# An S4D convolution and a SwiGLU FFN on one core: held loads, block 0's parameters apart, another instruction order

## The chip, the cores and the metric

The kernel runs on one core of a Trainium2 chip. The metric is the device time of one execution in microseconds (us), lower is better. A core has five engines that run on their own and meet at semaphores: TensorE (PE in the profile; its weight loads are PEld), VectorE (DVE), ScalarE (ACT), GpSimd (POOL) and SyncE (SP). Here SP only issues DMAs, and it issues all of them.

## The reference

Shapes: 2048 positions (L), 640 channels (D), 128 state pairs (N), FFN width 1728.

```python
def _A_ref(u, log_A_real, A_imag, C_real, C_imag, log_dt, D_skip):
    dt = jnp.exp(log_dt)
    A = -jnp.exp(log_A_real) + 1j * A_imag
    C = (C_real + 1j * C_imag) * dt[:, None]
    P = jnp.exp((A * dt[:, None])[:, :, None] * pos[None, None, :])
    K = 2.0 * jnp.einsum("dn,dnl->dl", C, P).real
    y = irfft(rfft(u_t, 2 * L) * rfft(K, 2 * L)[None], 2 * L)[:, :, :L]
    return y.transpose(0, 2, 1) + u * D_skip[None, None, :]

def _B_ref(x, w1, w3, w2):
    return (_silu(x @ w1) * (x @ w3)) @ w2

mod = (_silu(c) @ w_mod).reshape(1, 6, 1, -1)
sa, ca, ga, sb, cb, gb = (mod[:, i] for i in range(6))
h = _layernorm(x) * (1 + ca) + sa
x = x + ga * _A_ref(h, ...)
h = _layernorm(x) * (1 + cb) + sb
x = x + gb * _B_ref(h, B_w1, B_w3, B_w2)
```

## The kernel before

The channels are worked in five blocks of 128 (b = 0 to 4). For each block the kernel

- makes the tables of block b's phases on GpSimd (`t{b}.h.i`), and in eight chunks of 16 channels the convolution kernel's values: GpSimd adds the phases (`g{b}.{c}.ph`) and multiplies the magnitudes (`.z0` to `.z2`), ScalarE takes the sines (`.s0` to `.s4`), VectorE multiplies (`.m0` to `.m4`), TensorE sums over the state (`.p`, 32 fp32 products into `kps`), ScalarE copies the result out (`.r`), and VectorE adds the skip (`.d`)
- normalises the input (`h{b}.{i}.n`, on ScalarE or VectorE, four instructions of 128 x 128 for one of four tiles), multiplies and adds the modulation, and sends it through DRAM to another layout (`h{b}.f`)
- transforms both (`hh{b}.i.m` the input, `k{b}.i.m` the kernel; 16 products as the profile counts them, tile `ps`), applies the second step (`w{b}.i.f` and `.k`, tiles `fh` and `fk`), multiplies the spectra on VectorE (`.x0`, `.x1`, `.c`), and goes back (`z{b}.j.z`, tile `fz`), with a store of each part to the DRAM tensor `zd`.

Ahead of this stand the parameters: `in_log_ar`, `in_c_re`, `in_c_im`, `in_a_im` (128 partitions x 5 blocks x 128) are loaded whole, and VectorE and ScalarE make phases and magnitudes of them (steps `pa` for the phase, `pb` and `pc` for the magnitude and angle, `q` for the transposes). `al8{b}` multiplies a decay by 0 to 7, and `exp{b}` takes its exponentials.

All these steps are named tasks of one plan. `Plan.place` walks them with a cost for each and picks by rank. The ranks are the long table `RANKS`. A task may name two engines, and the plan takes the one that is to end first. The order that comes out is written into the program: each engine executes its instructions in exactly that order, SP its DMAs too. At most eight DMAs are in flight, since each waits for the one eight places ahead of it.

When the last chunk of block 4 is done, the task `change` frees the generator's pools, opens those of the FFN and loads the first 512 rows of x (`x2`, four DMAs of 320 KB) and a table `wd` (1 MB). Then `fw0` and `fw1` load the first two slices of FFN weights, `fs0` and `fs1` split them into two fp32r parts (ScalarE and VectorE), `iz0` and `iz1` load the back-transformed blocks 0 to 3, and `ir0` and `ir1` make the last step of the inverse transform for these rows (TensorE, then additions and statistics on VectorE). Block 4's part follows (`izb`), then the second layer norm, and the FFN: four groups of 512 rows, 14 slices each, every product in three fp32r products (`gu`, `acc`).

Of the kernel before, what the change touches and what calls it, by code (L numbers as in the profile page):

```python
# [18 lines left out]
P = 128  # L19
# [6 lines left out]
NB = 5  # L26
# [120 lines left out]
class InOrder:  # L147

    def __init__(self, k, eng):
        self.k, self.eng, self.prev = k, eng, None  # L150

    def __getattr__(self, name):
        f = getattr(self.eng, name)

        def g(*a, **kw):
            self.prev = self.k.order(f(*a, **kw), self.prev)  # L156
            return self.prev
# [120 lines left out]
class K:  # L278
# [534 lines left out]
    def run(self):  # L813
# [62 lines left out]
        z = {}  # L876
# [594 lines left out]
```

## Time and profile before

| | |
|---|---|
| median of three runs | 1010.73 us (1008.08 to 1012.32) |
| profiled execution | 1012.95 us, its span 1010.6 us |
| TensorE busy | 891.2 us, 88% of the span |
| VectorE busy | 656.8 us, 65% |
| ScalarE busy | 507.8 us, 50% |
| GpSimd busy | 279.4 us, 28% |
| DMA, over the span | 122.05 MB, mean 121 GB/s |

A row of groups reads: line, engine, operation, what it writes and reads, size, count | busy us, mean ns of one | idle time of the engine ahead of it, and who ended it. Since a helper records every operation, most rows have the helper's line, and it is the tile's name that tells them apart. A row of the timeline begins with the start and the duration in us; in brackets is the idle time before it and what ended it. A row of stretches has, for each engine, busy us and the number of instructions, then TensorE's granted clock (1.00 is full), the share of time that the DMA engines were busy, and GB/s.

### The profile page before, as it was taken

The numbers are of one execution on the slowest core, as the hardware profiler recorded it, in microseconds if no ns is written. First come the engines' busy times: TensorE is split into PE (matmuls) and PEld (weight loads), VectorE is DVE, ScalarE is ACT, GpSimd is POOL, SyncE is SP. The second block draws the span as 40 slices with busy tenths as digits, with TensorE's granted clock in tenths as the row PEclk, the third lists the DMA queues.
The fourth block names the chain that finished last, engine by engine and source line by source line (L and its number), as shares of the span: only waits on it lengthen the run. The fifth ranks groups of instructions, "written<-read, shape, count | busy, mean of one in ns | idle before, by whom it ended". The sixth has DMA issues, their size and how long they took to land.

```text
span 1010.6 us, 20260 instructions
## 1 busy us (share of the span) xinstructions
PE 891.2 (88%) x8129; PEld 714.0 (71%) x8129; DVE 656.8 (65%) x1214; ACT 507.8 (50%) x843; POOL 279.4 (28%) x288
## 2 busy tenths in 40 slices
PE   1463878788999885999999999999999999999996
PEld 1132756767887773677788888888888888888884
DVE  6998999999999475677664453464543643634332
ACT  6878787989787541432243343343433432533231
POOL 1798798988998200100000000000000000000000
PEclk9887998999999897899999999999999999999998
DMA  9955553624131759976232363332534333533302
GB/s 214 266 183 174 120 135 95 152 65 107 44 86 51 192 137 229 232 176 164 86 94 76 107 157 91 94 101 66 138 110 117 83 86 93 146 102 92 103 14 53
DMA packets 140998, 122.05 MB, mean 121 GB/s; under 512 B 13416, under 2 KB 124776, under 8 KB 139368
## 3 DMA queue, kind: packets, MB, share of 16 engines
q1 hardware_dynamic: 140904, 120.75, 45.4%
q8 instruction: 64, 1.05, 0.4%
q14 instruction: 30, 0.25, 0.1%
HBM read 99.75 MB, written 20.97 MB: 119 GB/s over the span
## 4 chain that ended last, share of the span: by engine, by line
PE 73%; DVE 12%; DMA 6%; ACT 3%; issue 3%; SPq 1%; POOL 0%; DVEq 0%; ACTq 0%; POOLq 0%
PE gu L753 12%; PE gu L754 12%; PE gu L755 12%; PE acc L788 6%; PE acc L789 6%; PE acc L790 6%; PE ps L156 4%; DVE yy L156 3%; PE fk L156 3%; PE kps L156 2%; PE fh L156 2%; DMA sp<-in_w_mod 2%; PE fz L156 2%; DVE fp L156 2%; PE iy L647 2%
## 5 line engine op out<-in xcount | busy, mean ns | idle before, releaser
L754 PE MATMUL gu<-xl,wh 128*128 128x512 f32 x540 | 212.6, 394 | 0.0
L753 PE MATMUL gu<-xh,wh 128*128 128x512 f32 x540 | 212.0, 393 | 0.5 <-ACT xh L683 0.5
L755 PE MATMUL gu<-xh,wl 128*128 128x512 f32 x540 | 211.7, 392 | 0.0
L658 ACT ACTIVATE wh<-wr 128x640 fp32r<-128x640 f32 x105 | 72.0, 732 | 136.3 <-PE gu L754 136.3
L721 POOL MEMSET w2l<- 64x640 f32 x3 | 1.9, 628 | 451.0 <-PE acc L789 451.0
L753 PEld LDWEIGHTS gu<-xh,wh 128*128 128x128 f32 x540 | 101.8, 188 | 25.6 <-issue 1.0
L754 PEld LDWEIGHTS gu<-xl,wh 128*128 128x128 f32 x540 | 101.9, 189 | 21.8
L755 PEld LDWEIGHTS gu<-xh,wl 128*128 128x128 f32 x540 | 101.8, 188 | 21.8
L788 PE MATMUL acc<-ah,w2h 128*128 128x512 f32 x260 | 103.8, 399 | 0.0
L789 PE MATMUL acc<-ah,w2l 128*128 128x512 f32 x260 | 102.2, 393 | 0.0
L768 DVE SCALAR_TENSOR_TENSOR a<-th,gu 128x512 f32<-128x512 f32 x52 | 35.8, 688 | 99.2 <-ACT th L767 99.0
L767 ACT ACTIVATE th<-gu 128x512 f32<-128x512 f32 x52 | 31.1, 598 | 135.4 <-PE gu L755 135.4
L769 DVE TENSOR_TENSOR a<-a,gu 128x512 f32<-128x512 f32 x52 | 35.7, 687 | 97.3 <-PE gu L755 97.2
L790 PE MATMUL acc<-al,w2h 128*128 128x512 f32 x260 | 96.5, 391 | 0.0
L156 POOL TENSOR_TENSOR yy<-e,e 128x512 f32<-128x512 f32 x80 | 86.3, 1095 | 16.6 <-PE kps L156 11.7
L659 DVE TENSOR_TENSOR wl<-wr,wh 128x640 fp32r<-128x640 f32 x105 | 82.2, 819 | 10.6 <-ACT wh L658 10.6
L156 POOL TENSOR_TENSOR ph<-p,p 128x1024 int32<-128x1024 int32 x40 | 79.0, 1975 | 7.3 <-ACT tr L156 6.6
L156 PE MATMUL kps<-yy,xx 128*32 128x64 f32 x2560 | 51.3, 234 | 31.3 <-DVE xx L156 23.4
L658 ACT ACTIVATE w2h<-w2r 128x640 fp32r<-128x640 f32 x51 | 37.6, 737 | 81.5 <-issue 42.6
L659 DVE TENSOR_TENSOR w2l<-w2r,w2h 128x640 fp32r<-128x640 f32 x51 | 42.0, 823 | 56.2 <-ACT w2h L658 56.0
L156 DVE TENSOR_TENSOR yy<-yy,tr 128x512 f32<-128x512 f32 (+1 forms) x80 | 75.5, 946 | 0.9 <-ACT tr L156 0.6
L156 PEld LDWEIGHTS kps<-yy,xx 128*32 128x32 f32 x2560 | 44.7, 116 | 41.2 <-issue 25.0
(204 smaller groups left out, 1646.6 us busy)
## 6 DMA issues: line engine op xcount, KB each, us to landing
wr<-in_w SPq DMA_DIRECT2D x104, 320.0 KB, 3.9
w2r<-in_w SPq DMA_DIRECT2D x52, 320.0 KB, 3.0
zd<-zt SPq DMA_DIRECT2D x40, 256.0 KB, 3.2
iz<-zd SPq DMA_DIRECT2D x24, 320.0 KB, 5.8
xs<-in_x SPq DMA_DIRECT2D x16, 320.0 KB, 11.4
hs<-hb SPq DMA_DIRECT2D x20, 256.0 KB, 2.4
xb<-hs SPq DMA_DIRECT2D x20, 256.0 KB, 4.8
x<-in_x SPq DMA_DIRECT2D x16, 320.0 KB, 11.0
```

The source lines that it names most:

```text
L156: self.prev = self.k.order(f(*a, **kw), self.prev)
L658: self.nc.scalar.activation(H, v, AF.Copy)
L659: eng.tensor_tensor(Lo, v, H.bitcast(F32), op=ALU.subtract)
L753: nc.tensor.matmul(pg, wh[:, i, k, :], xh[:, k, :], start=(k == 0), stop=False)
L754: nc.tensor.matmul(pg, wh[:, i, k, :], xl[:, k, :], start=False, stop=False)
L755: nc.tensor.matmul(pg, wl[:, i, k, :], xh[:, k, :], start=False, stop=(k == KT - 1))
L767: nc.scalar.activation(th, gu[0], AF.Tanh, scale=0.5)
L768: nc.vector.scalar_tensor_tensor(a, th, 1.0, gu[0], op0=ALU.add, op1=ALU.mult)
L769: nc.vector.tensor_mul(a, a, gu[1])
L788: nc.tensor.matmul(acc[k], w2h[:, sl], ah, start=(m == 0), stop=False)
L789: nc.tensor.matmul(acc[k], w2l[:, sl], ah, start=False, stop=False)
L790: nc.tensor.matmul(acc[k], w2h[:, sl], al, start=False, stop=(m == 12))
```

## The change

- The loads of `change`, `fw0` and `fw1` get a semaphore wait on the instruction of TensorE that stands last in the program at that point. `fw0` and `fw1` get a task of TensorE that they come after in the plan.
- The parameters of block 0 are loaded apart (`T0`, 64 KB each of three), `in_log_ar` behind them (`ll`), and the other blocks' after that (`T1`). The phase steps `pa`, which were made for all blocks at once, are made for block 0 and for blocks 1 to 4.
- The plan's cost of a norm on VectorE is 1.75 where it was 0.85; `.r` of the later chunks comes after the first chunk's.
- The table of ranks is another one, so the order on all engines is another one, and so is the choice of engine where a task has two.

```diff
@@ class InOrder
-        self.k, self.eng, self.prev = k, eng, None
+        self.k, self.eng, self.prev, self.behind = k, eng, None, None
...
             self.prev = self.k.order(f(*a, **kw), self.prev)
+            if self.behind is not None:
+                self.k.tc.add_manual_dep(self.prev.ins, self.behind.ins.name,
+                                         mybir.DependencyInfo(mybir.DependencyClass.Sync, mybir.DependencyReason.DATA), reason="behind")
             return self.prev
@@ params_begin
-        nc.sync.dma_start(self.la, self.log_ar.rearrange("(k p) n -> p k n", p=P))
@@ param_load
-            self.nc.sync.dma_start(T[nm], src.rearrange("(k p) n -> p k n", p=P)[:, bs])
+            self.nc.sync.dma_start(T[nm][:, bs], src.rearrange("(k p) n -> p k n", p=P)[:, bs])
@@ change
+            nc.sync.behind = nc.tensor.prev
             self.load_x2(0)
             nc.sync.dma_start(self.wd, self.t_wd)
+            nc.sync.behind = None
@@ run
-            add(f"fw{m}", "SP", 0, lambda m=m: split.__setitem__(m, self.weights_load(0, self.ORDER[m], self.wp)), ["change"], W + 5, dma=[327680] * 3)
+            add(f"fw{m}", "SP", 0, lambda m=m: load_w(m), ["change", f"k{b}.7.m" if m == 0 else f"z{b}.{m - 1}.z"], W + 5, dma=[327680] * 3)
...
+        def load_w(m):
+            nc.sync.behind = nc.tensor.prev
+            split[m] = self.weights_load(0, self.ORDER[m], self.wp)
+            nc.sync.behind = None
@@ gen_tasks
-            add(n + "r", "ACT", .27, ..., [n + "p"] + (...), t + 3, give=[("kg", n + "p")])
+            add(n + "r", "ACT", .27, ..., [n + "p"] + (...) + ([f"{g}.0.r"] if c else []), t + 3, give=[("kg", n + "p")])
@@ h_tasks
-            add(n + "n", ("ACT", "DVE"), (1.95, .85), ...
+            add(n + "n", ("ACT", "DVE"), (1.95, 1.75), ...
@@ param_tasks
-        a = chain("pa", self.param_steps(T, slice(0, NB))[0], NB, {0: ["dt", "T"], 3: ["lat0", "lat1"]}, prio + .2)
         for k, bs, n in both:
-            _, start, end = self.param_steps(cut(bs), bs)
-            b = chain(f"pb{k}.", start, n, {0: ["T"], 1: ["T"], 2: [f"pb{k}.0", f"pb{k}.1"]}, prio + k * later)
+            phases, start, end = self.param_steps(cut(bs), bs)
+            a = chain(f"pa{k}.", phases, n, {0: ["dt", f"T{k}"], 3: [f"lat{k}"]}, prio + .2 + k * later)
+            b = chain(f"pb{k}.", start, n, {0: [f"T{k}"], 1: [f"T{k}"], 2: [f"pb{k}.0", f"pb{k}.1"]}, prio + k * later)
@@ early_tasks
-        add("ld", "SP", 0, None, [], next(lp), dma=[2560, 327680, 2560])
-        add("T", "SP", 0, lambda: self.param_load(T, slice(0, NB)), [], next(lp), dma=[327680] * 3)
+        add("ld", "SP", 0, None, [], next(lp), dma=[2560, 2560])
+        add("T0", "SP", 0, lambda: self.param_load(T, one), [], next(lp), dma=[65536] * 3)
+        add("ll", "SP", 0, lambda: nc.sync.dma_start(self.la, self.log_ar.rearrange("(k p) n -> p k n", p=P)), [], next(lp), dma=[327680])
+        add("T1", "SP", 0, lambda: self.param_load(T, rest), [], next(lp), dma=[262144] * 3)
...
-        add("la", "ACT", .62, lambda: A.activation(self.la, self.la, AF.Exp), ["ld"], 1.0, table="exp")
+        add("la", "ACT", .62, lambda: A.activation(self.la, self.la, AF.Exp), ["ll"], 1.0, table="exp")
```

More of the change, by code (lines that the diff above doesn't have):

```diff
@@ L1084, in gen_tasks @@
                 take=[("kg", 1)], give=[("yy", n + "z0"), ("xx", n + "z2")])
-            add(n + "r", "ACT", .27, lambda c=c: rows(c), [n + "p"] + ([f"k{b - 1}.{i}.m" for i in range(8)] if b else ["exp0", "q0.t0", "q1.t0"]), t + 3, give=[("kg", n + "p")])
+            add(n + "r", "ACT", .27, lambda c=c: rows(c), [n + "p"] + ([f"k{b - 1}.{i}.m" for i in range(8)] if b else ["exp0", "q0.t0", "q1.t0"]) + ([f"{g}.0.r"] if c else []), t + 3, give=[("kg", n + "p")])
             add(n + "d", "DVE", .1, lambda c=c: skip(c), [n + "r"] + (["dsk"] if b == 0 else []), t + 3, give=[("kg", n + "p")])
@@ L1098, in h_tasks @@
             place = (lambda: self.pbank("hn")) if b else (lambda: self.psg.tile([P, 512], F32, name="hn", tag="f", bufs=3))
-            add(n + "n", ("ACT", "DVE"), (1.95, .85), lambda e, i=i, place=place: self.h_norm(b, i, place(), e), [n + "l", "hscale"], t, take=[(bank, 1)],
+            add(n + "n", ("ACT", "DVE"), (1.95, 1.75), lambda e, i=i, place=place: self.h_norm(b, i, place(), e), [n + "l", "hscale"], t, take=[(bank, 1)],
                 give=[("xq", n + "l")] if b else [])
@@ L1406, in early_tasks @@
             add(f"pr{g}", "PE", .9, lambda g=g: spread(g), ["m"], 21, take=[("f2", 1)], give=[("hz", "m")])
-            add(f"rw{g}", "ACT", .8, lambda g=g: keep(g), [f"pr{g}", "lat1", "pa4"], 21, give=[("f2", f"pr{g}")])
+            add(f"rw{g}", "ACT", .8, lambda g=g: keep(g), [f"pr{g}", "lat1", "pa0.4", "pa1.4"], 21, give=[("f2", f"pr{g}")])
         def fold():
```

131 rows, old and new, of the table RANKS are left out of this document.

## The prediction

> **What bounds the kernel now.** I read the page's busy shares first, then the stretches between five landmarks, then the timeline where a stretch looked odd. The landmarks: 11.1 us, where VectorE gets its last parameter load; 275; 344.6, in the last chunk of kernel spectra; 385, where the fourth and last inverse product of block 4 ends; 408.28, the FFN's first product.
>
> ```profile
> span 1010.6 us, 20260 instructions
> PE 891.2 (88%) x8129; PEld 714.0 (71%) x8129; DVE 656.8 (65%) x1214; ACT 507.8 (50%) x843; POOL 279.4 (28%) x288
> ...
> q8 instruction: 64, 1.05, 0.4%
> ```
>
> ```profile
> core 0: us, PE busy (x) PEld busy (x) DVE busy (x) ACT busy (x) POOL busy (x), PEclk, DMA share, GB/s
> 0.00:11.10 11.10, 1.30 (x5) 0.93 (x5) 3.75 (x20) 4.42 (x9) 1.68 (x19) 1.00 0.81 179
> 11.10:100.00 88.90, 40.55 (x628) 22.19 (x628) 82.25 (x151) 69.27 (x133) 64.24 (x60) 0.83 0.74 213
> 100.00:275.00 175.00, 144.22 (x2937) 121.39 (x2939) 167.64 (x317) 147.43 (x249) 154.02 (x154) 0.97 0.40 101
> 275.00:344.60 69.60, 68.66 (x1480) 57.58 (x1475) 64.38 (x116) 57.83 (x102) 54.40 (x51) 1.00 0.36 88
> 344.60:349.60 5.00, 0.62 (x6) 0.46 (x6) 0.00 (x0) 0.00 (x0) 0.00 (x0) 0.71 0.98 305
> 349.60:385.00 35.40, 32.68 (x363) 25.51 (x363) 23.61 (x50) 12.85 (x22) 0.63 (x1) 0.90 0.73 184
> 385.00:408.28 23.28, 10.13 (x46) 7.13 (x45) 12.17 (x42) 5.20 (x7) 1.27 (x1) 0.63 0.86 205
> 408.28:1010.60 602.32, 593.03 (x2676) 478.82 (x2676) 303.02 (x522) 210.81 (x323) 3.16 (x4) 0.99 0.40 107
> ```
>
> The FFN's 602.32 us are TensorE's, 593.03 busy, and the diff leaves its code alone; everything is decided in the first 408.28. From 11.1 to 275 VectorE is busy 249.89 of 263.90 us: it binds. From 275 to 344.6 TensorE is busy 68.66 of 69.60: it binds there. In the next 5 us every engine stands while the transfers run at 98%.
>
> **The stall and the held loads.**
>
> ```profile
> 331.47 1.09 PE L156 MATMUL ps<-wk,ks 128*64 128x128 f32 x16
> ...
> 337.56 2.10 SPq L156 DMA_DIRECT2D x<-in_x  x4
> ...
> 340.17 1.13 SPq L156 DMA_DIRECT2D wr<-in_w  x2
> ...
> 343.45 1.14 PE L156 MATMUL kps<-yy,xx 128*32 128x64 f32 x60
> ...
> 348.98 0.64 PE L156 MATMUL kps<-yy,xx 128*32 128x64 f32 x4 [4.39 <-issue]
> 349.54 5.64 PE L156 MATMUL ps<-wk,ks 128*64 128x128 f32 x64
> ...
> 352.17 3.11 SPq L156 DMA_DIRECT2D iz<-zd  x4
> ```
>
> ```profile
> DMA packets 1287, 2.15 MB, mean 155 GB/s; under 512 B 96, under 2 KB 1120, under 8 KB 1120
> ## 3 DMA queue, kind: packets, MB, share of 16 engines
> q1 hardware_dynamic: 1287, 2.15, 65.6%
> ```
>
> ```profile
> q8 instruction: 1, 0.02, 2.6%
> ```
>
> TensorE stops after 60 of 64 products whose operands are all there, for "issue": nothing that the profile shows. The second fence is the DMA view from 332.5 to 346.4 us: no instruction packet at all. The third is the same view from 346.4 to 349: one packet, and TensorE goes on. On the page 8129 products and 8129 weight loads share 64 such packets, 254 each. So I read the stall as a late fetch: the loads for the FFN, issued from 337.56 on, hold back the next 16 KB of TensorE's instructions. Its price is 4.39 us, and 64 products after it take 5.64 where 16 took 1.09, so 4.36: 1.28 more at the lower clock (0.71 in that stretch). Together 5.7.
>
> In the new order the loads of `change` wait for product `k4.6.m`, the first behind that chunk: without the stall 344.59 + 1.09 = 345.7, or 8.1 us later than 337.56. Counting 256 instructions per packet from the stall, the boundary that hurt now falls 37 instructions ahead of the chunk's end, so that fetch is out about 1.4 us before the loads. The next boundary comes with `w4.1.k`, six groups of 16 products behind the loads' start, some 6 us by the row with 1.09. A fetch that waits until the old one's time (346.4 is 8.8 after 337.56) is back 3 us later, against 256 instructions in hand, eight such groups or 8.7 us. So -5.7; at the other end nothing (a rival below).
>
> What is queued behind: SP issues in order, so `wd`, `fw0` (held again for `w4.0.f`), `fw1` (for `w4.3.k`), two stores of `z4.0` and the loads `iz0` and `iz1` all stand behind the held ones. VectorE's `fs0` and TensorE's `ir0` wait for them.
>
> ```profile
> 364.77 0.69 DVE L156 TENSOR_TENSOR fp<-fk,hz 128x512 f32<-128x512 f32 x1 [0.30 <-PE fk L156]
> ...
> 368.01 1.35 ACT L156 ACTIVATE wh<-wr 128x640 fp32r<-128x640 f32 x2
> ...
> 375.51 0.67 DVE L156 TENSOR_TENSOR x<-iy,x 128x512 f32<-128x512 f32 x1
> ...
> 380.45 4.56 PE L156 MATMUL fz<-fp,wz 64*128 64x512 f32 x16
> ...
> 408.28 0.79 PE L753 MATMUL gu<-xh,wh 128*128 128x512 f32 x1 [0.48 <-ACT xh L683]
> ```
>
> ```profile
> wd<-in_t_wd SPq DMA_DIRECT2D x1, 1024.0 KB, 10.7
> wr<-in_w SPq DMA_DIRECT2D x2, 320.0 KB, 11.7
> ```
>
> The first weights, issued from 340.17 and 11.7 in flight, land about 352.4, 14.8 after the first load, and are first read at 368.01: 15.6 of slack. Holding takes 8.1 of it, and a tail earlier by the 4.4 takes more; about 3 is left. `ir0` now stands behind `w4.7.k`, later than before. I cost the tail at -0.5, from -2 (VectorE's pause around 375.51 goes) to +3 (`fs0` waits).
>
> **VectorE's work up to there.** By the built order 24 of 52 norm instructions move from VectorE to ScalarE, the products `al80` and `al81` move to GpSimd, three evictions come to VectorE, and five parameter operations are split in two.
>
> ```profile
> L156 DVE TENSOR_SCALAR hn<-xq,rs_y_h,rs_n_h 128x128 f32<-128x128 f32 x44 | 18.2, 413 | 1.2
> L156 ACT ACTIVATE hn<-xq,rs_n_h,rs_y_h 128x128 f32<-128x128 f32 x20 | 9.2, 462 | 3.5 <-DMA xq<-in_x 2.5 <-DVE fp L156 0.4
> L156 DVE TENSOR_TENSOR ks<-al,j 128x1024 f32<-128x1024 f32 x1 | 1.2, 1219 | 0.0
> L156 DVE TENSOR_TENSOR xs_al<-al,j 128x1024 f32<-128x1024 f32 x1 | 2.8, 2826 | 0.0
> L156 POOL TENSOR_TENSOR al<-al,j 128x1024 f32<-128x1024 f32 x3 | 5.9, 1966 | 0.0
> L156 DVE COPY sp<-ps 128x512 f32<-128x512 f32 x19 | 12.7, 685 | 3.0 <-PE ps L156 2.9
> L156 DVE TENSOR_TENSOR xb<-e 128x512 f32<-128x512 f32 x3 | 2.2, 722 | 0.0
> L156 DVE TENSOR_TENSOR xb<-e 128x128 f32<-128x128 f32 x3 | 0.9, 286 | 0.0
> ...
> L156 DVE TENSOR_TENSOR e<-e,dt 128x640 f32<-128x640 f32 x1 | 0.8, 824 | 3.8 <-DMA e<-in_a_im 3.8
> ```
>
> Norms: 24 x 0.413 = -9.9. Products: -(1.22 + 2.83) = -4.05. Evictions: 3 x 0.685 = +2.05. Splits: 5 x (0.722 + 0.286 - 0.824) = +0.9. Sum -11.0 us of VectorE's work. It costs ScalarE 24 x 0.462 = 11.1 and GpSimd 2 x 1.97 = 3.9; from 11.1 to 344.6 these are busy 274.5 and 272.7 of 333.5, so both fit, though waits behind them may grow.
>
> The Trainium skill, "SBUF — State Buffer", "SBUF: two separate sides", says that a GpSimd operation and a VectorE operation on two SBUF inputs exclude each other for a whole instruction. By it the two moved products still block VectorE for 3.9 us, and the sum would be -7.1 instead of -11.0. The trace bears part of it out, since one shape took 1.22 us and once 2.83.
>
> The last row is the start: VectorE waits 3.79 us for `in_a_im`. Block 0's 64 KB pieces now come first, and its five phase and four magnitude operations fill that wait: 9 x 0.286 = -2.6 (0 to -3.8), after which VectorE again waits for the last load, now block 1 to 4's. So -13.6 if VectorE alone set the time. But from 275 on TensorE binds, and what is saved behind that point doesn't count: summing the groups' means along both orders, VectorE's work up to the fifth chunk of block 3 (its product is at 272 us) is 4.7 less, and 9.3 less at the last chunk. So -7.3 is the near end, -13.6 the far end; with TensorE 99% busy I take -9.
>
> **Sum.** -9 - 5.7 - 0.5 = -15.2. The profiled execution took 1012.95 us (span 1010.6 and 2.35 around it): 997.7. It lies 2.2 above the median 1010.73 of the three runs, inside their spread; I forecast 997 us.
>
> **Rivals.** *VectorE alone* (0.15): ScalarE and GpSimd keep up and TensorE's work is spread forward: -13.6 - 5.7 - 2 = 991.7. For it: 79.1 us of idle TensorE between 11.1 and 275. Against: 0.94 us of it from 275 to 344.6.
>
> *The stall stays* (0.13): it was no fetch, or the next fetch falls into the burst: 1012.95 - 9.5 = 1003.4. For it: a cause that no record names. Against: the packet that arrives with the restart. The Trainium skill, "Runtime: NRT & Kernel Launch", "Instruction fetch mechanics", would have it so: it gives 16 KiB blocks of 256 instructions, which agrees with 254 per packet, but 2048 instructions of buffer for TensorE and a cost mostly hidden. By that depth 14 us without a packet would do no harm (2955 instructions in the 69.6 us before); the row with 4.39 speaks against it.
>
> *The order gives nothing* (0.12): VectorE, in order, waits behind ScalarE for eight tiles' norms of 4 x 0.462 = 1.85 each, 14.8 against the 13.6 saved: -5.7 - 0.5 + 1.2 = 1008.0. Against: the norms' multiplies stand some instructions behind them.
>
> *The held loads set the end* (0.07): from first load to FFN is 408.28 - 337.56 = 70.7 us now. If these were the transfers' (share 0.73 and 0.86), the FFN would start at 345.7 + 70.7 - m = 416.4 - m, m the gain ahead of it: 8.1 later less m. With the start's 2.6 alone that is +5.5: 1018.5. It decides once the weights land over 3 us later than reckoned, so that `fs0` blocks VectorE.
>
> **How the numbers follow.** The forecast itself has 0.53. Over 0.5% (5 us, about what a measurement here can tell) faster are it, VectorE alone, and the stall's staying: 0.81; to this 0.02 of the third rival's spread: 0.83. Same 0.10, slower 0.07. The range runs from 989 (the far ends, less the 2.2 to the median) to 1006 (between the second and third rival).
>
> **What would show it.** VectorE's 3.8 us wait for `in_a_im` gone; no `issue` row above 2 us on TensorE near the last chunk; the first FFN product at about 393; the FFN 602 as before. It is wrong if that product comes after 404, if `fs0` waits for a DMA, or if an equal stall shows among `fh` and `fk`.

## The result, and the profile after

The changed kernel takes 1015.89 us (median of nine runs, 1013.34 to 1020.63), the kernel before 1012.44 in the runs beside it (1008.08 to 1014.78): a ratio of 1.0042, 95% interval [1.0026, 1.0059]. It is 0.4% slower, where 1.5% faster was forecast; the time lies above the range of 989 to 1006. The profiled execution took 1015.55 us, its span 1013.7.

The page and the stretches first. The landmarks are the ones of before: the last load of the parameters (11.1), 275, the end of the last chunk's product (351.9), the end of block 4's last inverse product (386.8), the time just ahead of the FFN's first product (410.15; it starts at 410.19).

```profile
span 1013.7 us, 20265 instructions
PE 897.3 (89%) x8129; PEld 715.3 (71%) x8129; DVE 649.2 (64%) x1195; ACT 520.0 (51%) x867; POOL 284.1 (28%) x291
```

```profile
0.00:11.10 11.10, 1.51 (x6) 1.14 (x6) 6.95 (x28) 5.94 (x11) 3.25 (x20) 1.00 0.77 178
11.10:100.00 88.90, 43.83 (x647) 24.57 (x651) 79.86 (x151) 73.45 (x137) 69.61 (x66) 0.82 0.75 220
100.00:275.00 175.00, 142.33 (x2798) 117.72 (x2800) 154.68 (x284) 147.52 (x256) 147.51 (x148) 0.91 0.39 98
275.00:351.90 76.90, 75.28 (x1622) 64.16 (x1620) 69.27 (x123) 64.09 (x113) 58.66 (x54) 1.00 0.25 64
351.90:386.80 34.90, 29.60 (x346) 20.85 (x346) 23.30 (x49) 12.85 (x22) 0.63 (x1) 0.92 1.01 262
386.80:410.15 23.35, 10.76 (x46) 7.31 (x44) 12.14 (x42) 5.20 (x7) 1.27 (x1) 0.65 0.86 206
410.15:1013.70 603.55, 594.03 (x2676) 479.58 (x2676) 302.99 (x522) 210.97 (x323) 3.17 (x4) 0.99 0.39 107
```

Three things are to be seen. VectorE's 656.8 us of work have become 649.2, which is 7.6 less where 11.0 less was reckoned. The stretch of 5 us in which every engine stood is gone. And between 100 and 275 us VectorE is busy only 154.68 of 175 us, where it was 167.64, and TensorE does 2798 products where it did 2937: what VectorE saved turned into idle time, and TensorE fell behind by 139 products there (up to 100 us it was 19 ahead).

The timeline around the last chunk, TensorE and SP, and the FFN's start:

```profile
350.68 1.17 PE L157 MATMUL kps<-yy,xx 128*32 128x64 f32 x64
351.79 2.84 PE L157 MATMUL ps<-wk,ks 128*64 128x128 f32 x48
...
352.96 1.74 SPq L157 DMA_DIRECT2D x<-in_x  x4
...
367.40 1.35 ACT L157 ACTIVATE wh<-wr 128x640 fp32r<-128x640 f32 x2
...
410.19 0.79 PE L757 MATMUL gu<-xh,wh 128*128 128x512 f32 x1 [0.49 <-ACT xh L687]
```

The 64 products of the last chunk run in one piece, and the next 48 follow at once: the 4.39 us gap is gone. But the last chunk starts at 350.68 where it started at 343.45. That is 7.2 us later, in a part that was to come 9 us earlier; the rest of the way is as forecast to about 1 us.

What ended VectorE's waits from 11 to 340 us, in the changed kernel (us in total, times, the longest):

```profile
DVE ks L157 <- PE kps L157: 7.0, 5, 1.8
DVE yy L157 <- ACT tr L157: 3.5, 6, 1.5
DVE ks L157 <- ACT ks L157: 3.5, 5, 1.2
DVE cols L157 <- PE pv L157: 3.4, 1, 3.4
DVE sp L157 <- PE ps L157: 2.4, 2, 1.4
DVE xb L157 <- ACT wb L157: 2.2, 1, 2.2
```

The same view of the kernel before, and then the whole stretch, the kernel before first:

```profile
DVE e L156 <- DMA e<-in_a_im: 3.8, 1, 3.8
DVE ks L156 <- PE kps L156: 3.1, 3, 1.4
DVE sp L156 <- PE ps L156: 2.9, 2, 2.5
```

```profile
11.00:340.00 329.00, 248.84 (x4880) 197.12 (x4882) 313.41 (x579) 272.06 (x478) 272.67 (x263) 0.94 0.47 127
11.00:340.00 329.00, 249.53 (x4773) 194.97 (x4775) 296.53 (x546) 275.51 (x489) 274.60 (x265) 0.90 0.46 125
```

Before, VectorE waited 15.6 us in all there (329 less 313.41 busy), 3.8 of it for `in_a_im`. Now it waits 32.5 (329 less 296.53), 1.4 of it for a load (`xq`) and most of it for TensorE and ScalarE, at many places.

TensorE's granted clock is lower too, 0.90 in this stretch where it was 0.94, and that is a rival cause. It does not order the kernels, though: of the kernels below, `hold_al` has 0.90 as well and starts its last chunk 4.2 us before the changed kernel, and `hold_norm` has 0.92 and starts it 4.1 us after it. What the lower clock costs by itself no run here shows.

### The profile page after: what moved, and what is told of

It reads as the page before. It is cut to its first block, busy times and chain, and to the rows that moved or that the text cites. A ratio compares the mean times of both kernels' runs of the same rounds, so it can differ in the third digit from the quotient of the medians.

```text
span 1013.7 us, 20265 instructions
## 1 busy us (share of the span) xinstructions
PE 897.3 (89%) x8129; PEld 715.3 (71%) x8129; DVE 649.2 (64%) x1195; ACT 520.0 (51%) x867; POOL 284.1 (28%) x291
## 4 chain that ended last, share of the span: by engine, by line
PE 66%; DVE 12%; DMA 7%; ACT 6%; issue 3%; POOL 3%; SPq 1%; ACTq 0%; DVEq 0%; POOLq 0%
PE gu L757 12%; PE gu L758 12%; PE gu L759 12%; PE acc L792 6%; PE acc L793 6%; PE acc L794 6%; DVE fp L157 3%; DVE yy L157 3%; DMA xs<-in_x 3%; PE ps L157 2%; ACT tr L157 2%; PE iy L651 2%; DVE xx L157 2%; DVE fk L157 2%; PE kps L157 1%
## 5 line engine op out<-in xcount | busy, mean ns | idle before, releaser
L662 ACT ACTIVATE w2h<-w2r 128x640 fp32r<-128x640 f32 x51 | 37.6, 738 | 81.5 <-issue 42.5
```

Of the source, the lines that this page charges most:

```text
L662: self.nc.scalar.activation(H, v, AF.Copy)
```

## The experiments

Times in the text below are ratios to the kernel before as it ran beside the kernel in question, with the 95% interval; the changed kernel's is 1.0042 [1.0026, 1.0059]. 0.1% is 1.0 us.

**The holds alone.** `hold_old` is the kernel before with the holds of the change and nothing else; `nohold_new` is the changed kernel without them.

```diff
 hold_old: kernel before
+            nc.sync.behind = nc.tensor.prev
             self.load_x2(0)
             nc.sync.dma_start(self.wd, self.t_wd)
+            nc.sync.behind = None
... the same around weights_load of fw0 and fw1
 nohold_new: changed kernel
-            nc.sync.behind = nc.tensor.prev
```

> The old order, with nothing changed but that the loads of `change`, `fw0` and `fw1` wait for the last product ahead of them in the program (k4.1.m, the first group behind the last chunk, for `change`). Theory (late fetch: the loads' burst held TensorE's next instructions back): the 4.39 us gap after 60 of 64 products is gone and the 64 products behind it run at the full clock, 4.4 + 1.3 = 5.7, of which the held loads may take back up to 1: 5 us faster than the kernel before, ratio 0.995. Rival 1 (the gap has another cause): it stays, ratio 1.000. Rival 2 (held loads set the end): the gap is gone, but VectorE's `fs0` waits for the weights, and the first FFN product comes no earlier: 1.000 to 1.002.

> The changed kernel without the holds: the loads of `change`, `fw0` and `fw1` go out as soon as their space is free, everything else as in the changed kernel. Theory (late fetch): the loads go out some 8 us earlier, ahead of the last chunk's end, and the block of instructions that is due at 346.6 or 352.1 comes late: a gap of 3 to 5 us without a cause in the records, 4 to 6 us slower than the changed kernel, ratio to the kernel before 1.008 to 1.010. Rival 1 (in the new order no block falls into the burst, the holds do nothing): as the changed kernel, 1.004. Rival 2 (the holds cost the tail): 1 to 3 us faster than the changed kernel, 1.001 to 1.003.

Measured: `hold_old` 0.9962 [0.9942, 0.9981], `nohold_new` 1.0061 [1.0036, 1.0087]. The timeline of `hold_old`, then that of `nohold_new`:

```profile
343.46 1.17 PE L156 MATMUL kps<-yy,xx 128*32 128x64 f32 x64
344.56 3.71 PE L156 MATMUL ps<-wk,ks 128*64 128x128 f32 x64
...
345.73 1.90 SPq L156 DMA_DIRECT2D x<-in_x  x4
...
402.72 0.72 PE L756 MATMUL gu<-xh,wh 128*128 128x512 f32 x1 [1.08 <-ACT xh L686]
```

```profile
340.24 2.10 SPq L157 DMA_DIRECT2D x<-in_x  x4
...
349.34 0.92 PE L157 MATMUL kps<-yy,xx 128*32 128x64 f32 x45
352.21 0.55 PE L157 MATMUL kps<-yy,xx 128*32 128x64 f32 x19 [1.95 <-issue]
```

The DMA view of `nohold_new` from 340 to 349 us, and then from 349 to 352.3:

```profile
q1 hardware_dynamic: 1288, 2.16, 100.7%
```

```profile
q8 instruction: 1, 0.02, 2.0%
```

With the loads held, 64 products follow the last chunk in 3.71 us where they took 5.64, and the FFN starts at 402.72 where it started at 408.28: 5.56 us in the profiled pair, 3.8 (1.9 to 5.9) by the runs. Without the hold the gap comes back in the new order, after 45 of 64 products, while the queue of loads is full and no instruction packet moves; it ends after one has. 19 products and as many weight loads are left then: 38 instructions, and the prediction had counted 37. The gap is 1.95 us there, not the 3 to 5 expected: this packet moved at 349.78, 0.5 us before TensorE ran out at 350.26, where in the kernel before it moved at 346.49, 1.9 us after TensorE had run out. In `hold_old`, with the same order as the kernel before, this packet (the 39th of 64 in all four kernels) moves at 341.44, 5.0 us earlier. So the late fetch is shown from both sides. The difference of `nohold_new` to the changed kernel, 0.2%, agrees with 1.95 us, though the intervals overlap.

**Which stretch of the new order loses.** In the kernels from here on the order is written out as a list of tasks with their engines. `splice_g07` has the new list up to block 0's last chunk and then the old one; `old_to_180` and `old_to_220` go over to the new list again later; `late_old` has the new list up to 254 us. All have the holds.

```diff
 splice_g07
-new
+new[to g0.7.p] + old[what is left]
 old_to_180, old_to_220
+splice_g07[to h3.1.o or g2.5.s3] + new[what is left]
 late_old
+new[to g3.2.m3] + old[what is left]
```

> The changed kernel's order up to block 0's last chunk (its product g0.7.p, 107 us), and from there the old order, with its choice of engines (norms on VectorE again), held loads kept. Theory (the new order loses its time in blocks 1 and 2, between 107 and 225 us): block 0 ends 0.9 us ahead of the kernel before, the old pace follows, and the stall is gone: 1012.4 - 0.9 - 5 = 1006.5, ratio 0.994. Rival (what is lost was made ready in the first 107 us, by what is pushed behind it): the loss stays, ratio 1.002 to 1.004.

> Order of splice_g07 (new up to block 0's last chunk, 107 us, then old) up to the place where both orders have done nearly the same, some 180 us (h3.1.o), and from there the new order. Theory (TensorE saturated from 225 us on in all of these kernels, so the FFN's start follows the number of products that it has behind it at 225: 2591 in the kernel before, 2450 in the changed one, 141 x 0.058 = 8.2 us; 136 of them are lost from 100 to 140): the loss is avoided, as splice_g07, ratio 0.997 to 0.999. Rival (the new order loses its time behind 180, whatever stands ahead): 1.002 to 1.004.

> As old_to_180, but the old order runs on to some 220 us (g2.5.s3), and the new order follows from there. Theory (what is behind TensorE at 225 decides): as splice_g07, 0.996 to 0.998. Rival (VectorE's waits in the new order behind 225, where it is in the chain of waits up to 336 us, cost it): 1.000 to 1.004.

> The new order up to 254 us (g3.2.m3), where both orders have done the same tasks but one, and from there the old one. Theory (the products lacking at 225 decide): as the changed kernel, 1.003 to 1.005. Rival (the new order loses behind 254): 0.998 to 1.001.

Measured: `splice_g07` 0.9973 [0.9961, 0.9986], `old_to_180` 1.0044 [1.0027, 1.0061], `old_to_220` 1.0054 [1.0028, 1.0081], `late_old` 1.0013 [0.9996, 1.0031]. Going over to the old order at 107 us recovers 0.7% of the changed kernel's time, and comes within 0.1% of `hold_old`: up to there the new order loses nothing that shows. My theory of TensorE's backlog at 225 us fell: with the old order up to 180 or 220 us the end is as late as in the changed kernel. The stretches from 180 to 200 and 200 to 225 us show how, `hold_old` first, then `old_to_180`:

```profile
180.00:200.00 20.00, 15.36 (x322) 14.10 (x320) 19.68 (x38) 17.57 (x28) 16.42 (x19) 0.91 0.60 148
200.00:225.00 25.00, 20.50 (x392) 15.72 (x390) 23.03 (x44) 19.22 (x34) 21.34 (x20) 0.93 0.16 44
```

```profile
180.00:200.00 20.00, 8.19 (x202) 7.77 (x201) 11.09 (x19) 17.15 (x28) 15.21 (x17) 0.66 0.49 111
200.00:225.00 25.00, 20.40 (x336) 17.05 (x334) 20.77 (x40) 18.30 (x36) 15.83 (x15) 0.80 0.35 93
```

At the seam TensorE and VectorE both stand (8.19 and 11.09 of 20 us busy), and then keep the lag. The seams so cost time of their own, and these cuts can't say which stretch of the new order loses; `late_old`, whose seam falls where both lists have done the same but for one task, puts some 0.3% of it behind 254 us, though its interval overlaps the changed kernel's.

**Chunk products earlier, skips later.** Two attempts at the waits themselves, and a control. The two lists with skips moved differ from their bases in more than was meant.

```diff
 prod_early: changed kernel, places of seven tasks
+g1.0.p behind hh0.1.m; g2.0.r, g2.1.r behind k1.4.m
+g2.0.d, g2.1.d, g2.2.p behind g2.2.m4; g2.3.p behind g2.3.m4
 skips_late: changed kernel, places of .r and .d (most 2 to 10 us later), and of other tasks
+g1.1.d behind h2.1.a (was w0.0.x0); g1.3.d behind g1.6.m0 (was w0.2.c)
...
 skips_old: splice_g07, treated in the same way
```

> The changed kernel with three chunk products earlier in TensorE's order, since they start 9.2 (g1.0.p), 8.8 (g2.2.p) and 9.8 us (g2.3.p) after their operands are there: g1.0.p behind hh0.1.m, g2.2.p ahead of w1.0.f, g2.3.p behind w1.0.k, and the copies and skips of g2.0 and g2.1 that free their bank ahead of them. Theory (the new order puts products late; GpSimd stands 6.59 and 2.65 us for their buffers, and VectorE waits for kps 3.9 us longer than before the change): most of the 6.5 us that the main phase lost comes back, 4 to 7 us faster than the changed kernel, ratio to the kernel before 0.997 to 1.000. Rival (TensorE's backlog is the same, another wait takes the place): as the changed kernel, 1.003 to 1.005.

> The changed kernel with only the copies `.r` (ScalarE, 0.37 us) and skips `.d` (VectorE, 128x4, 0.16 us) of the chunk products at other places, most of them 2 to 10 us later; work, engines and all other places as before. Theory (VectorE's saved 11 us are spent in waits of its fixed order: from 11 to 340 us it is idle 32.5 us in the changed kernel and 14.9 in hold_old, and 10.6 of that stand ahead of the skips, for a chunk product that TensorE has not made or ScalarE not copied): most of those 10.6 go, 5 to 8 us faster than the changed kernel, ratio to the kernel before 0.996 to 0.999. Rival (the wait only moves to the next instruction that needs TensorE or ScalarE): 1.002 to 1.005.

> The control: the same treatment of copies and skips in the order of splice_g07 (new up to 107 us, then old), where VectorE stands 7.2 us ahead of the skips. Theory (it is the new order that has its skips too early): at most 4 us faster than splice_g07 (0.9973), 0.993 to 0.997, so less than skips_late gains. Rival (moving skips is worth the same anywhere, nothing in it is of the new order): as much as skips_late against its own base.

Measured: `prod_early` 1.0053 [1.0034, 1.0073], `skips_late` 1.0064 [1.0051, 1.0077], `skips_old` 1.0065 [1.0049, 1.0080]. No gain; `skips_old` is even 0.9% slower than `splice_g07`. But neither of these two moves copies and skips alone, as was meant. In the list of `skips_late` 19 of VectorE's 200 multiplications `.m`, 13 of GpSimd's 160 `.ph` and `.z` and 15 of TensorE's 220 groups of products also stand at other places; in `skips_old` it is 17, 12 and 9. So these two are no test of the skips, and `skips_old` is no control. `prod_early` moves its seven tasks and nothing else. GpSimd's longest wait near 210 us, in the changed kernel and in `prod_early` (timeline):

```profile
213.09 2.09 POOL L157 TENSOR_TENSOR yy<-e,e 128x512 f32<-128x512 f32 x2 [6.59 <-PE kps L157]
```

```profile
217.65 1.95 POOL L172 TENSOR_TENSOR ph<-p,p 128x1024 int32<-128x1024 int32 x1 [5.90 <-ACT tr L172]
```

VectorE's waits in `skips_late` from 11 to 340 us:

```profile
DVE yy L171 <- POOL yy L171: 6.7, 9, 1.5
DVE ks L171 <- ACT ks L171: 4.9, 6, 1.3
DVE yy L171 <- ACT tr L171: 4.1, 7, 1.2
```

In `prod_early` GpSimd's 6.59 us for TensorE became 5.90 for ScalarE, at a later `ph`. In `skips_late` the 10.5 us ahead of VectorE's skips became 4.9, and its wait for GpSimd's `yy` rose from 1.6 to 6.7; idle in all is 33.9 us where it was 32.5. Which of the moved tasks did this, the run can't say. What `prod_early` shows is that a long wait in front of one instruction doesn't say that this instruction is in the wrong place.

**Longer rearrangements.** Tables, and everything up to the last chunk, by durations taken from the traces.

```diff
 tables_moved: changed kernel, places of t, al, mag, exp, and of other tasks
+exp1 behind g0.5.r (was g0.5.s4); exp2 behind g1.2.r (was g1.3.s2)
...
 resorted: tasks, holds and split parameters of the changed kernel, another list
```

> The changed kernel with only the phase tables `t`, `al`, `mag` (GpSimd) and the exponentials `exp` (ScalarE, 3.94 us at a stretch) at other places, and all else as it was: exp1 6 to 8 us later, exp2 at 137 us instead of 133.6 (it stands ahead of w0.2.h, for which TensorE waits 3.58 us), block 1's and 3's tables shifted. Theory (the loss is waits of engines that execute in order, and long instructions at the wrong place make them): 3 to 7 us faster than the changed kernel, 0.997 to 1.001. Rival (only VectorE's own places count): 1.003 to 1.005.

> The tasks, held loads and split parameters of the changed kernel, but all tasks up to block 4's last chunk sorted anew with each task's duration taken from the two traces (not the plan's costs), and the choice of engine too. Theory (nothing but the places costs the time: VectorE's work is 11 us less and could be used): VectorE's idle time from 11 to 340 us falls from 32.5 to about 15, 10 to 20 us faster than the changed kernel, ratio 0.985 to 0.994. Rival (work, clock or transfers bind, and a better order finds nothing): 0.996 to 1.004.

Measured: `tables_moved` 1.0200 [1.0185, 1.0215], `resorted` 1.0160 [1.0143, 1.0177]. My theory fell here too. VectorE's idle time rose to 44.7 and 40.7 us. `tables_moved` isn't a move of tables alone either: 23 of the 200 `.m`, 13 of the 160 `.ph` and `.z` and 13 of ScalarE's 200 sines stand elsewhere too, so its loss can't be put down to the tables. `resorted`, sorted by durations from the traces, is no better than the changed kernel's list but 1.2% slower; what such sorting leaves out I didn't find.

**The parts of the change in the old order.** Here engines change and the places stay, so these runs price the parts. `norm_dve` takes the norms back in the new order; the others bring one part each into `hold_old`, at the old places.

```diff
 norm_dve: changed kernel;  hold_norm: hold_old, the other way round
-h0.1 h0.2 h1.1 h2.2 h2.3 h3.2 h4.0 h4.3 .n@ACT, h0.3 h4.1 .n@DVE
+h0.1 h0.2 h1.1 h2.2 h2.3 h3.2 h4.0 h4.3 .n@DVE, h0.3 h4.1 .n@ACT
 hold_al: hold_old
-al80@DVE al81@DVE
+al80@POOL al81@POOL
 hold_start: block 0's parameters apart
+new[to g0.0.ph] + old[what is left]
 hold_all: hold_start with the engines of hold_norm, al81@POOL
 hold_norm_h0: hold_old
-h0.1.n@DVE h0.2.n@DVE h0.3.n@ACT
+h0.1.n@ACT h0.2.n@ACT h0.3.n@DVE
 hold_norm_rev: hold_old
-h0.0 h0.3 h1.3 h2.0 h3.0 h4.1 h4.2 .n@ACT
+h0.0 h0.3 h1.3 h2.0 h3.0 h4.1 h4.2 .n@DVE
```

> The changed kernel's order, but every input norm on the engine that it had before (ten of twenty tiles change, six more of them on VectorE: 24 x 0.413 = 9.9 us of work back on it, 11.1 off ScalarE). Theory (the move is a real saving, VectorE is in the chain up to 336 us): 5 to 9 us slower than the changed kernel, ratio 1.009 to 1.013. Rival (norms on ScalarE hold up the sines behind them, VectorE's longer waits for ACT and ScalarE's own lag eat the saving): as the changed kernel or faster, 0.999 to 1.005.

> hold_old (old order, held loads) with nothing changed but the engine of ten input norms, as the new order has it: eight tiles from VectorE to ScalarE, two back, so 24 x 0.413 = 9.9 us off VectorE and 11.1 us onto ScalarE, all at the old places. Theory (VectorE binds up to 275 us, the saving is worth its size there, and the new order loses it by its places): 5 to 9 us faster than hold_old, ratio to the kernel before 0.987 to 0.991. Rival (ScalarE is as near to its limit, and VectorE, in order, waits behind 1.85 us of norm each time): 0.995 to 1.002.

> hold_old with nothing changed but that the products al80 and al81 (1.22 and 2.83 us of VectorE) are GpSimd's. Theory (VectorE binds): 2 to 4 us faster than hold_old, 0.992 to 0.994. Rival (their time is covered by VectorE's waits for hscale, or GpSimd's two products of 1.97 us hold up the phases of the next chunks): 0.996 to 1.000.

> Block 0's parameters apart and the new order up to block 0's first phases (g0.0.ph, 7 us earlier than before), and from there the old order, with held loads. Theory (the 2.6 us that VectorE gains at the start are kept): 2 to 3 us faster than hold_old, 0.993 to 0.995. Rival (the start is not on the path: the last rows of x and the statistics, up to hscale, end later or no earlier): 0.996 to 0.999.

> hold_start with hold_norm's engines and al81 on GpSimd: every part of the change but its order behind block 0's first phases. Theory (savings of VectorE's work add up where the places are good): the sum of the three, 8 to 13 us faster than hold_old, 0.984 to 0.989, and faster than both kernels. Rival (fixed places, then waits in place of work): 0.995 to 1.003.

> hold_old with block 0's part of hold_norm alone: the norms h0.1 and h0.2 on ScalarE, h0.3 on VectorE, 1.65 us off VectorE in all. Theory (the chain through the engines is tight all the way, a lag made at 90 us stays): the 3.4 us that hold_norm's trace lost there arrive at the end, ratio to the kernel before 0.9985 to 1.0005. Rival (later slack takes it up, only the norms of blocks 2 to 4 count): as hold_old, 0.995 to 0.997.

> hold_old with the opposite move: the seven tiles' norms that the old order has on ScalarE go to VectorE, at the same places: 28 x 0.413 = 11.6 us more on VectorE, 12.9 less on ScalarE. Theory (each order is made for its engines, and a move either way costs): 5 to 11 us slower than hold_old, ratio 1.001 to 1.007. Rival (ScalarE's time is the dearer one everywhere): faster than hold_old, 0.986 to 0.995.

Measured, with the start of the last chunk's product in the profile (343.46 in `hold_old`, 350.68 in the changed kernel):

| kernel | ratio to the kernel before | last chunk starts, against `hold_old` |
|---|---|---|
| `hold_old` | 0.9962 [0.9942, 0.9981] | |
| `hold_start` | 1.0021 [1.0005, 1.0036] | +5.2 us |
| `hold_al` | 0.9975 [0.9956, 0.9993] | +3.1 |
| `hold_norm` | 1.0082 [1.0058, 1.0105] | +11.3 |
| `hold_all` | 1.0085 [1.0065, 1.0104] | +13.4 |
| `hold_norm_h0` | 1.0013 [1.0000, 1.0026] | +5.6 |
| `hold_norm_rev` | 1.0071 [1.0048, 1.0094] | +11.7 |
| changed kernel | 1.0042 [1.0026, 1.0059] | +7.2 |
| `norm_dve` | 1.0130 [1.0100, 1.0159] | +17.9 |

The last column compares single executions: `hold_old`'s took 1.0 us less than its median, `hold_al`'s 2.2 and `hold_all`'s 3.3 more. Where the columns differ by a few us, the ratio counts.

9.9 us of work taken off VectorE make the old order 1.2% slower. The waits of `hold_norm` (11 to 340 us) name the place (the same three are 1.2, 0.6 and 0.8 us in `hold_old`):

```profile
DVE ks L171 <- ACT ks L171: 6.5, 3, 3.0
DVE hn L171 <- ACT hn L171: 4.9, 5, 2.0
DVE xx L171 <- ACT tr L171: 4.9, 5, 1.9
```

and its timeline shows one norm at work, ScalarE and VectorE, with the same place in `hold_old` below it:

```profile
75.81 1.94 ACT L171 ACTIVATE hn<-sp,rs_n_h,rs_y_h 128x128 f32<-128x128 f32 x4
77.68 0.36 ACT L171 ACTIVATE ks<-kps 128x256 f32<-128x256 f32 x1
...
78.08 0.17 DVE L171 TENSOR_TENSOR ks<-kps,dsk 128x4 f32<-128x4 f32 x1 [2.95 <-ACT ks L171]
```

```profile
73.81 1.75 DVE L156 TENSOR_SCALAR hn<-sp,rs_y_h,rs_n_h 128x128 f32<-128x128 f32 x4
75.08 0.38 ACT L156 ACTIVATE ks<-kps 128x256 f32<-128x256 f32 x1 [0.40 <-PE kps L156]
...
75.49 0.17 DVE L156 TENSOR_TENSOR ks<-kps,dsk 128x4 f32<-128x4 f32 x1
```

In the old order the norm runs on VectorE beside ScalarE's sines and copies, and the copy comes at 75.08. On ScalarE the norm's 1.94 us stand ahead of the copy, VectorE comes to the skip and waits 2.95 us for it: more than the 1.75 it was spared. Nothing makes up for it later. `hold_norm_h0` has this at block 0 alone, and the 5.6 us of lag in its profile are still 0.5% at the end. The opposite move costs as much: 11.6 us more on VectorE, 11.7 us later at the last chunk. In the new order the norms on ScalarE are worth 0.9%, or 8.9 us (`norm_dve`), as was expected there. So each order fits its own engines, and in these runs a move that isn't followed by new places costs, either way.

## Why the prediction was wrong

*The stall and the held loads* were right. The forecast of 5.7 us is `hold_old`'s 5.56 between the profiles, and inside the interval of its runs (1.9 to 5.9), near its upper end. The Trainium skill, "Runtime: NRT & Kernel Launch", "Instruction fetch mechanics", with its 2048 instructions of buffer for TensorE and a cost mostly hidden, doesn't agree: `nohold_new` stalls 1.95 us where the count of 256 puts a boundary, 12.1 us after the packet before. What the change earns by the hold in its own order is the smaller 1.95, since there the boundary falls elsewhere.

*The tail* came within its bounds: from the end of the last chunk's products to the FFN 351.86 to 410.19 is 58.3 us, before 349.62 to 408.28 58.7. The 1.28 us of slow products that the forecast counts with the stall lie in that stretch as well, so the tail itself is some 0.9 longer, where -0.5 (-2 to +3) was forecast. The weights are split from 367.40 on and nothing waits for their loads; the rival of late loads has no place.

*VectorE's work* was counted right in what moves (the 24 norm instructions and both products are gone from it), 3.4 us too large in the sum (-7.6 over the span for -11.0), and wrongly priced. This is the step that failed: "with TensorE 99% busy I take -9", between a near end of -7.3 and a far end of -13.6. In its place the runs show +7.2. I took an engine busy 249.89 of 263.90 us for one whose work sets the time, so that work taken off it comes back as time. But the 24 x 0.413 went to an engine that stands in the same chain: the profile's waits of VectorE were for ScalarE and TensorE already, and `hold_norm` shows +11.3 for the -9.9. That ScalarE was busy only 274.5 of 333.5 us said that the work fits, not that it fits at that place. The sentence "waits behind them may grow" had no number, and neither end of the term allowed for a loss.

The runs take the change apart in two ways. From `hold_old`, the engines of the norms, both products and the start at the old places cost 1.2% (`hold_all`), and the rest, the new order with its 45 other evictions on the other engine, wins 0.4% back. Or the new order with the old engines of the norms is 1.7% slower than `hold_old` (`norm_dve`), and the norms' move then wins 0.9%, near the 9.9 us at which their work was counted. So the price of the same move has another sign in another order, and the forecast put the cost of the new places at nothing.

*The start* was wrong: -2.6 was forecast, `hold_start` shows +5.2. The 3.8 us wait for `in_a_im` is gone, as forecast, and block 0's first phases are ready at 30.7 where it was 37.6. The loss belongs to the old places behind it, though: `splice_g07`, with the new order up to 107 us, is within 0.1% of `hold_old`, so the changed kernel doesn't lose its time at the start. The rows below, the groups of VectorE in the changed kernel, show what came in place of the wait:

```profile
L157 DVE TENSOR_TENSOR e<-e,dt 128x512 f32<-128x512 f32 x1 | 2.1, 2076 | 0.6 <-DMA e<-in_a_im 0.6
L157 DVE TENSOR_TENSOR xb<-xb,wb 128x512 f32<-128x512 f32 x1 | 1.6, 1641 | 2.2 <-ACT wb L157 2.2
```

a 2.2 us wait for ScalarE's arctangent for blocks 1 to 4, whose chain now begins later, and operations that GpSimd's earlier work stretches: `e<-e,dt`, 512 wide, takes 2.08 us beside `al80` (9.53 to 11.48 on GpSimd), where 640 wide took 0.82. The row scales of the norms (`hscale`) so end at 72.6 us where they ended at 68.5, and they, not the first phases, release block 0's norms.

*The two products on GpSimd* (-4.05) earn nothing that shows: `hold_al` 0.9975 against 0.9962. The rule weighed there (the Trainium skill, "SBUF — State Buffer", "SBUF: two separate sides") has VectorE blocked for their 3.9 us, and the row of `e<-e,dt` agrees, 1.3 us of it; the rest of the missing 4.05 isn't explained.

*Of the rivals*, "the order gives nothing" had the mechanism, VectorE in order behind ScalarE's norms, and 14.8 us for it, but it was priced against 13.6 saved and given 0.12. It is the saving that isn't there: with the norms, both products and the start at the old places the last chunk is 13.4 us late in the profile and the kernel 1.2% slower than `hold_old` (`hold_all`). No rival combined a cured stall with a main phase that is slower. *The signs* named ahead: the wait for `in_a_im` and the issue gap are gone, as said; the first FFN product at 410.2 instead of 393, and "wrong if it comes after 404" is what came; the FFN takes 603.55 where it took 602.32.

What stays open is which places of the new order cost the time, and how much of it is the lower clock. Three chunk products moved earlier don't cure it (`prod_early`); no run here names the place where the sum is made.

## What to carry to other kernels

Where four engines execute fixed lists and wait for each other, work moved off the busiest one is worth what the waits behind its new place allow, and that can be less than nothing, or more in one order than in another: price the move by the instruction on the receiving engine that now comes later, and by who waits for it. A stall without a cause in the records is worth its size when the cause is known, and it can be had alone: `hold_old`, with the holds in the old order, has the lowest ratio of all these kernels, 0.4% ahead of the kernel before and 0.8% ahead of the changed one. So take the parts of a change one at a time, measure an order again after each, and compare the lists that a trial is built from before reading its time: three of these trials moved more than they were meant to.

## What the runs showed of the hardware

A packet of TensorE's instructions moved late while the queue of loads was full (5.0 us later in the kernel before than in `hold_old`). The gap was 4.39 us in the kernel before and 1.95 in `nohold_new`, and none in `hold_old` and the changed kernel, whose loads are held. From the packet's start to TensorE's next product it was 2.5 and 2.4 us (346.49 to 348.98, 349.78 to 352.21).

Some of VectorE's operations stretch while GpSimd computes, up to about GpSimd's end. In `hold_start`'s timeline, VectorE above and GpSimd below:

```profile
26.73 1.24 DVE L172 TENSOR_SCALAR h_nm<-h_nm 128x4 f32<-128x4 f32 x1
...
35.17 2.43 DVE L172 TENSOR_TENSOR xb<-xb 128x512 f32<-128x512 f32 x1
```

```profile
24.78 3.16 POOL L172 TENSOR_TENSOR p<-p,step 128x256 int32<-128x256 int32 x2 [5.01 <-DVE step L172]
...
34.93 2.13 POOL L172 TENSOR_TENSOR ph<-p,p 128x1024 int32<-128x1024 int32 x1
```

The first takes 0.17 us in `hold_old`, the second 0.76. Both end close behind GpSimd's operation (27.97 against 27.94, 37.60 against 37.06). Most operations don't stretch: the 80 `xx<-tr,xx` take 683 ns each in both kernels, with GpSimd busy 272.67 and 274.60 of 329 us. The Trainium skill, "SBUF — State Buffer", "SBUF: two separate sides", has the two engines exclude each other for a whole instruction, VectorE's with two SBUF inputs or in a mode of two ports; the second row has two inputs and agrees, and of the first, with one, no run here shows the mode.
